# Batch 0's attention placed alone ahead of the products, and the packing of batches 1 to 3 placed inside them

## The chip, the cores and the metric

The kernel runs on one core of one Trainium2 chip. The metric is the device time of one execution in microseconds (us); smaller is better. Engines are named as in the profile: PE (matrix products), DVE (VectorE), ACT (ScalarE), POOL (GpSimd), SP (the queue that issues the DMAs).

## The reference

For 8 batches of 8 heads, 576 positions and 64 channels, an attention in two steps, and behind it two feed-forward layers on the 4608 rows of 512 channels:

```python
def sm_attn(qq, kk, vv):
    s = scale * np.matmul(qq, kk.transpose(0, 1, 3, 2))
    ...
    a = np.exp(s)
    a = a / (np.sum(a, axis=-1, keepdims=True) + 1e-09)
    return np.matmul(a, vv)
p_packed = sm_attn(p, k, v)               # 32 packed positions
out = sm_attn(q, p_packed, p_packed)      # 576 positions out of 32
...
rms = np.sqrt(np.mean(x * x, axis=-1, keepdims=True) + 1e-06)
g = (x / rms * rms_g) @ w_gate
x = (g * sigmoid(g)) * ((x / rms * rms_g) @ w_val) @ w_out
a, b = x @ w1, x @ w2
return (a * b @ w3) @ w_out2
```

(The last lines are put together from two functions; `sigmoid` stands for the expression written out there. The four weights of the second layer and the three of the first arrive as 64-bit floats.)

## The kernel before

**Three stages.** The first runs the attention and the gate and value products of the first layer, batch by batch. The second and third do the products behind them; the change touches nothing there. What moves lies in the first stage, in the first 190 us.

**Pieces of a batch's attention.** `pack(b)` (line 174 on) is the first attention. It is a generator of seven pieces, each ended by `yield`: the scores `k` by `pTs` (L186), maximum (L190) and exponential (L193) of one half of the heads; the same of the other half; the transposes of the exponentials (L202) with the copies into `a1T` (L203 on ACT, L204 on DVE) and the reciprocals of the sums (L205, L206); the product with `v` (L213) and the load of the next `v`; the scaling (L221); a transpose (L225) with the copies into `bdP1T` (L229) and `gP1T` (L231); the small products of `bdP1T` with itself (L239) with four copies into `bdG` (L244). `unpack(b)` is the second attention in eighteen pieces: scores from `q` and `bdP1T` (L267), DVE transposes (L271), maximum, subtraction and exponential (L277 to L280), sums and their reciprocals (L283 to L285), a multiplication on POOL (L286), transposes back into `a2T` (L290), products with `bdG` (L297) and the squares (L300), a sum on POOL (L303), its reduction over partitions by a product with `ones` (L309, read by L311), the reciprocal root `rinv` on POOL (L314, L315), its spread (L320), the scaling of `a2T` (L323) and the split of `a2T` into a rounded part `ah` (L59, ACT) and a remainder `al` (L60, DVE).

**Weights.** `gvw` converts the 24 tiles of the gate and value weights from 64-bit floats, one tile to a step: two operations on ACT (L112, L113), two on DVE (L115 makes `c_t`, L116 writes `wgv`), one on POOL (L118), and a load for the tile three steps ahead (L103). A group g of 256 columns is four tiles; `wb_unit(b, g)` (L342, with its split into `wbh` on ACT and `wbl` on DVE) needs them.

**Products.** `dense_units(b)` is 48 units of six matrix products each (L380) for batch b, with `th` (L386 on ACT, L387 on DVE), `vl` (L391, ACT) and `ht` (L392, POOL) behind them; `wb_unit` for the next group stands behind units 3, 11, 19 and so on. The first unit of batch b needs `ah` and `al` of `unpack(b)` and group 0 of the weights.

**What sets the order.** Each engine works through its own queue in program order, and the program order is written out by hand. In the front, a string names which generator moves on: `p` (pack), `u` (unpack), `c` (a weight tile), `w` (the first `wb_unit`), `l` (loads for later). After it, `planned` runs the 48 units of a batch and moves the other generators on at the unit numbers given in lists: `PACK`, `UNPACK` and one for the weight steps. In the front stand `pack(0)`, `pack(1)`, `unpack(0)` and twelve weight steps; in batch b's products `pack(b + 2)` and `unpack(b + 1)`, in those of batch 0 also the other twelve weight steps, and from batch 1 on five steps a batch of `ow`, the conversion of later weights.

**PSUM.** All pieces of the attention and `wb_unit` share two slots of two banks (`slot("at")`); L380 has four banks of its own (`gv`).

## Time and profile before

| | |
|---|---|
| median of 3 runs | 1374.38 us (1374.08 to 1375.65) |
| the profiled execution | 1373.85 us, its span 1372.1 us |
| mean granted clock of PE | 0.983 |
| PE busy | 1319.5 us, 96% of the span |
| DVE, ACT, POOL busy | 62%, 42%, 44% |

The page is of one execution of the program. Busy time of PE is modelled from pipelined instructions, so a busy PE is not PE at its peak. `x16` behind a row is the number of instructions in it; a product in 32-bit floats counts as two, so L186's 16 products of `pack` are 32 in the trace. An idle time in square brackets stands ahead of the instruction, with what ended it.

### The profile page before, as it was taken

The page shows a single profiled execution, that of the slowest core. Times are in us where ns is not written, and L with a number is a line of the kernel's source. Part 1 is how long each engine was busy: PE and PEld are TensorE (multiplying, and loading weights), DVE is VectorE, ACT ScalarE, POOL GpSimd, SP SyncE. Part 2 cuts the span into 40 slices and gives each one's busy share as a digit, 9 for nine tenths or more (in the row PEclk, how much of TensorE's full clock was granted, in tenths as well). Part 3 has the DMA queues.
Part 4 walks back from the last instruction along what each step waited for, and adds up shares of the span by engine and source line. Part 5 has one row for each costly group of instructions (what it writes and reads, how often), then busy time and mean ns, then how long its engine had stood idle before and what let it go on. Part 6 is the DMA issues. An engine that isn't in the chain of part 4 may idle for free.

```text
span 1372.1 us, 23271 instructions
## 1 busy us (share of the span) xinstructions
PE 1319.5 (96%) x8800; PEld 1118.3 (82%) x8800; DVE 854.9 (62%) x1308; ACT 574.3 (42%) x1093; POOL 608.0 (44%) x524
## 2 busy tenths in 40 slices
PE   4479999999999999999999999999999999999998
PEld 1368888888888888888888888888888888899998
DVE  4787676866867557745376464566467457557444
ACT  2465665655656666534244343015005103304113
POOL 2456556555555653212132113447345544545543
PEclk7699999999999999999999999999999999999999
DMA  9763666564543457743299884756755855787875
GB/s 311 278 242 93 220 208 215 192 193 152 175 146 109 140 178 257 258 144 123 74 334 384 337 303 167 265 207 201 283 194 198 280 209 193 244 311 254 280 269 183
DMA packets 86688, 301.94 MB, mean 220 GB/s; under 512 B 9520, under 2 KB 14640, under 8 KB 72624
## 3 DMA queue, kind: packets, MB, share of 16 engines
q1 hardware_dynamic: 86576, 300.46, 63.3%
q8 instruction: 69, 1.13, 0.3%
q14 instruction: 43, 0.35, 0.1%
HBM read 223.87 MB, written 76.55 MB: 219 GB/s over the span
## 4 chain that ended last, share of the span: by engine, by line
PE 87%; DVE 5%; issue 1%; DMA 1%; POOL 1%; ACT 1%; SPq 0%; ACTq 0%; DVEq 0%; POOLq 0%
PE gv L380 20%; PE gv L878 13%; PE at L878 13%; PE at L567 12%; PE gv L567 7%; PE gv L972 6%; PE at L972 6%; PE gv L668 3%; PE at L342 3%; PE at L297 1%; DVE wgv L116 1%; PE at L213 1%; DMA hr<-hT_d 1%; DVE wbl L60 1%; PE at L309 1%
## 5 line engine op out<-in xcount | busy, mean ns | idle before, releaser
L392 POOL TENSOR_TENSOR ht<-th,vl 128x288 f32<-128x288 f32 x192 | 163.3, 859 | 109.4 <-ACT vl L391 50.0
L380 PE MATMUL gv<-ah,wbh 128*128 128x288 f32 x768 | 175.2, 309 | 2.4 <-ACT vl L391 2.0
L380 PE MATMUL gv<-ah,wbl 128*128 128x288 f32 x768 | 164.7, 296 | 1.8 <-DVE wbl L60 1.8
L380 PE MATMUL gv<-al,wbh 128*128 128x288 f32 x768 | 164.6, 295 | 0.0
L380 PEld LDWEIGHTS gv<-ah,wbh 128*128 128x128 f32 x768 | 121.8, 189 | 50.8 <-issue 24.1
L60 DVE TENSOR_TENSOR hl<-hr,hh 128x512 fp32r<-128x512 f32 x108 | 100.5, 936 | 76.8 <-ACT hh L59 74.7
L904 POOL TENSOR_TENSOR s<-uc 128x512 f32<-128x512 f32 (+1 forms) x40 | 49.0, 1224 | 219.5 <-DVE uc L860 219.5
L118 POOL TENSOR_TENSOR c_o<-c_o,c_y 128x512 int32<-128x512 int32 x52 | 70.8, 1362 | 166.3 <-DVE c_o L116 103.7
L878 PE MATMUL gv<-xh,w 128*128 128x512 f32 (+1 forms) x560 | 137.7, 367 | 0.0
L878 PE MATMUL at<-xh,w 128*128 128x512 f32 (+1 forms) x560 | 137.7, 367 | 0.0
L380 PEld LDWEIGHTS gv<-ah,wbl 128*128 128x128 f32 x768 | 123.3, 188 | 2.9 <-DVE wbl L60 2.9
L380 PEld LDWEIGHTS gv<-al,wbh 128*128 128x128 f32 x768 | 123.6, 189 | 0.0
L387 DVE SCALAR_TENSOR_TENSOR th<-th,gv 128x288 f32<-128x288 f32 x192 | 85.2, 445 | 55.6 <-ACT th L386 51.4
L59 ACT ACTIVATE hh<-hr 128x512 fp32r<-128x512 f32 x108 | 67.7, 629 | 116.3 <-PE at L567 61.0
L878 PEld LDWEIGHTS gv<-xh,w 128*128 128x128 f32 x560 | 102.5, 188 | 13.4
L878 PEld LDWEIGHTS at<-xh,w 128*128 128x128 f32 x560 | 102.5, 188 | 13.3
L567 PE MATMUL at<-hl,wo_h 128*128 128x512 f32 x288 | 112.1, 389 | 0.0
L567 PE MATMUL at<-hh,wo_l 128*128 128x512 f32 x288 | 112.1, 389 | 0.0
L567 PE MATMUL at<-hh,wo_h 128*128 128x512 f32 x288 | 112.0, 389 | 0.0
L391 ACT ACTIVATE vl<-gv 128x288 f32<-128x288 f32 x192 | 79.1, 412 | 75.7 <-PE gv L380 57.0
L386 ACT ACTIVATE th<-gv 128x288 f32<-128x288 f32 x192 | 79.1, 412 | 49.2 <-PE gv L380 47.0
L60 POOL TENSOR_TENSOR xl<-yi,xh 128x1024 fp32r<-128x1024 f32 (+1 forms) x20 | 52.1, 2607 | 74.3 <-ACT xh L59 50.8
(156 smaller groups left out, 2812.7 us busy)
## 6 DMA issues: line engine op xcount, KB each, us to landing
w<-ws_d SPq DMA_DIRECT2D x40, 1024.0 KB, 5.5
w<-w_d SPq DMA_DIRECT2D x35, 1024.0 KB, 4.8
w<-ws_d SPq DMA_DIRECT2D x40, 768.0 KB, 5.9
hT_d<-ht SPq DMA_DIRECT2D x96, 288.0 KB, 3.3
hr<-hT_d SPq DMA_DIRECT2D x108, 256.0 KB, 4.7
w<-in_w_gv_dram SPq DMA_DIRECT2D x24, 512.0 KB, 7.7
w<-in_w_out_dram SPq DMA_DIRECT2D x20, 512.0 KB, 4.7
v<-in_v_dram SPq DMA_DIRECT2D x8, 1152.0 KB, 7.7
```

Of the source, the lines that this page charges most:

```text
L59: nc.scalar.activation(out=hi, in_=src, func=AF.Copy)
L60: eng_lo.tensor_tensor(out=lo, in0=src, in1=hi.bitcast(F32), op=ALU.subtract)
L118: nc.gpsimd.tensor_tensor(out=d, in0=d, in1=shape(y), op=ALU.add)
L380: nc.tensor.matmul(t[:, :HALF], lhsT=w[:, e, 256 * i + 128 * f:256 * i + 128 * f + 128], rhs=x[:, e, HALF * hf:HALF * hf + HALF], start=(n ...
L386: nc.scalar.activation(out=th, in_=t[:, :HALF], func=AF.Tanh, scale=0.5)
L387: nc.vector.scalar_tensor_tensor(out=th, in0=th, scalar=1.0, in1=t[:, :HALF], op0=ALU.add, op1=ALU.mult)
L391: nc.scalar.activation(out=vl, in_=t[:, :HALF], func=AF.Copy, scale=0.5)
L392: nc.gpsimd.tensor_tensor(out=ht[:, hf], in0=th, in1=vl, op=ALU.mult)
L567: nc.tensor.matmul(acc[m], lhsT=w[:, kk, 128 * m:128 * m + 128], rhs=x, start=(kk == 0 and a == 0), stop=(kk == NF - 1 and a == 2))
L878: nc.tensor.matmul(t, lhsT=wi[:, r, pos, a], rhs=x[:, j, r, :w], start=(start and at == 0), stop=(at == 5), skip_group_check=True)
L904: nc.gpsimd.tensor_tensor(out=s2, in0=u2, in1=c22, op=ALU.mult)
L972: nc.tensor.matmul(t, lhsT=wi[:, s, k, 128 * m:128 * m + 128], rhs=x, start=(j in (0, 5, 4, 3) and k == 0 and n == 0), stop=(k == 3 and n ...
```

## The change

Seven things change; what is computed stays the same.

The front's string now moves only `pack(0)`, `unpack(0)`, the first `wb_unit`, the later loads and eight weight steps. `pack(1)` stands in batch 0's products at units 0 to 14, `unpack(1)` behind it at units 13 to 44, and sixteen weight steps at every second unit from 2 to 33. Batch 1's products hold `pack(2)`, `unpack(2)` and `pack(3)` and two steps of `ow`. From batch 2 on, `pack(b + 2)` and `unpack(b + 1)` stand at the same units as before, with six steps of `ow` instead of five.

Copies move: the four into `bdG` from DVE to ACT, and for all batches but 0 the one of `a1T`'s first half too. In `pack`, the reciprocals of the sums stand ahead of the copies. The load of batch 0's `v` is issued ahead of the first three weight tiles. `ones` holds 1/512, so that the mean comes out of L309 and one POOL operation (L314) is gone. An exponential of two elements at the very start brings the load of ACT's table there.

```diff
+    nc.gpsimd.memset(ones, 1.0 / DM)
+    nc.scalar.activation(out=ones[:, 1:], in_=ones[:, :1], func=AF.Exp)
+    nc.gpsimd.memset(ones, 1.0 / DM)
...
-        nc.scalar.activation(out=a1T[:, 1], in_=ts[1][:TP, :R * 128], func=AF.Copy)
-        nc.vector.tensor_copy(a1T[:, 0], ts[0][:TP, :R * 128])
         nc.vector.tensor_scalar(out=rs, in0=rs, scalar1=1e-9, scalar2=None, op0=ALU.add)
         nc.vector.reciprocal(out=rs, in_=rs)
+        if b:
+            nc.scalar.activation(out=a1T[:, 0], in_=ts[0][:TP, :R * 128], func=AF.Copy)
+        else:
+            nc.vector.tensor_copy(a1T[:, 0], ts[0][:TP, :R * 128])
+        nc.scalar.activation(out=a1T[:, 1], in_=ts[1][:TP, :R * 128], func=AF.Copy)
         yield
...
-            nc.vector.tensor_copy(bdG[c0, b % 2, :, c0], t[c0, :, :NP])
+            nc.scalar.activation(out=bdG[c0, b % 2, :, c0], in_=t[c0, :, :NP], func=AF.Copy)
...
-                                scalar1=0.0, scalar2=1.0 / DM, op0=ALU.max, op1=ALU.mult)
-        yield
-        nc.gpsimd.tensor_scalar(out=ssq, in0=ssq, scalar1=1e-6, scalar2=None, op0=ALU.add)
+                                scalar1=0.0, scalar2=1e-6, op0=ALU.max, op1=ALU.add)
+        yield
...
+    load_v(0)
     next(gvw)
-    load_v(0)
     load_q(0)
...
-    front = dict(p=chained(pack(0), pack(1)), u=unpack(0), c=gvw, w=wb_first(), l=later())
-    for x in "pp c c p c pp c pp u c u u p u p u c w u u u c u uu p u c uu l pp c uu c uu pp c l c c":
+    front = dict(p=pack(0), u=unpack(0), c=gvw, w=wb_first(), l=later())
+    for x in "ppp c p c pp u c p uuuu uu u c u c u u w u c u c u l c uuuu":
...
+            others = [([0, 0, 4, 8, 10, 12, 14], pack(1)),
```

**DVE at the start, from batch 0's maxima to the scores of its second attention.** The names: `c_t` and `wgv` are one weight tile's conversion, `p_` the scaled rows, `bdP1T` what the second attention's scores wait for. Before:

```order
L190 TENSOR_REDUCE mx<-at 128x1
L191 TENSOR_SCALAR nb<-mx 128x1
L115 TENSOR_SCALAR c_t<-c_h 128x512
L116 SCALAR_TENSOR_TENSOR wgv<-c_h,c_t 128x2x256
L115 TENSOR_SCALAR c_t<-c_h 128x512
L116 SCALAR_TENSOR_TENSOR wgv<-c_h,c_t 128x2x256
L204 COPY a1T<-at 96x768
...
L221 TENSOR_SCALAR p_248<-at,rs 128x64 x2
L115 TENSOR_SCALAR c_t<-c_h 128x512
L116 SCALAR_TENSOR_TENSOR wgv<-c_h,c_t 128x2x256
L229 COPY bdP1T<-at 64x4x32 x2
```

and now:

```order
L192 TENSOR_REDUCE mx<-at 128x1
L193 TENSOR_SCALAR nb<-mx 128x1
L205 TENSOR_SCALAR rs<-rs 128x2
L206 RECIPROCAL rs<-rs 128x2
L210 COPY a1T<-at 96x768
L115 TENSOR_SCALAR c_t<-c_h 128x512
L116 SCALAR_TENSOR_TENSOR wgv<-c_h,c_t 128x2x256
L115 TENSOR_SCALAR c_t<-c_h 128x512
L116 SCALAR_TENSOR_TENSOR wgv<-c_h,c_t 128x2x256
L226 TENSOR_SCALAR p_240<-at,rs 128x64 x2
L234 COPY bdP1T<-at 64x4x32 x2
```

The copy of `a1T` moved ahead of two conversions, and no conversion stands any more between the scaled rows and `bdP1T`, where the fourth tile stood.

**PE from the scores of batch 0's second attention to the first products of `dense_units(0)`.** Before:

```order
L267 MATMUL at<-q,bdP1T 32x288 x16
L186 MATMUL at<-k,pTs 32x288 x16
L342 MATMUL at<-wgv,gP1T 32x512 x8
L297 MATMUL at<-a2T,bdG 128x288 x4
L202 MATMUL at<-ident,e_319 96x128 x12
L309 MATMUL at<-ones,sq 96x2 x6
L213 MATMUL at<-v,a1T 32x64 x48
L320 MATMUL at<-ident,rinv 128x96 x6
L225 MATMUL at<-ident,p_499 128x128
L239 MATMUL at<-bdP1T 32x32 x8
L380 MATMUL gv<-ah,wbh 128x288 x2
```

and now (line numbers have shifted by up to seven):

```order
L272 MATMUL at<-q,bdP1T 32x288 x16
L244 MATMUL at<-bdP1T 32x32 x8
L302 MATMUL at<-a2T,bdG 128x288 x4
L346 MATMUL at<-wgv,gP1T 32x512 x8
L314 MATMUL at<-ones,sq 96x2 x6
L324 MATMUL at<-ident,rinv 128x96 x6
L384 MATMUL gv<-ah,wbh 128x288 x2
```

Batch 1's five steps (scores, transposes, product with `v`, transpose, small products) left the stretch, and with the last two of them went what stood directly ahead of the first products.

**DVE in the first units of batch 0's products.** Before:

```order
L387 SCALAR_TENSOR_TENSOR th<-th,gv 128x288
L271 STREAM_TRANSPOSE a_600<-at 128x2x288 x2
L277 TENSOR_REDUCE mx_601<-a_600 128x18
L115 TENSOR_SCALAR c_t<-c_h 128x512
L116 SCALAR_TENSOR_TENSOR wgv<-c_h,c_t 128x2x256
L387 SCALAR_TENSOR_TENSOR th<-th,gv 128x288
L279 TENSOR_TENSOR a_600<-a_600,mx_601 128x576
```

and now:

```order
L391 SCALAR_TENSOR_TENSOR th<-th,gv 128x288
L115 TENSOR_SCALAR c_t<-c_h 128x512
L116 SCALAR_TENSOR_TENSOR wgv<-c_h,c_t 128x2x256
L391 SCALAR_TENSOR_TENSOR th<-th,gv 128x288
L226 TENSOR_SCALAR p_683<-at,rs 128x64 x2
L115 TENSOR_SCALAR c_t<-c_h 128x512
L116 SCALAR_TENSOR_TENSOR wgv<-c_h,c_t 128x2x256
```

Here `pack(1)` is at work in the place of `unpack(1)`, and a conversion stands between nearly any two `th`.

## Rows read from the trace of the kernel before

**Rows 1.** The page, 40 slices of the span: busy tenths of PE.

```profile
PE   4479999999999999999999999999999999999998
```

**Rows 2.** Windows: stretch, length, busy PE, PEld, DVE, ACT, POOL; clock, DMA share, GB/s.

```profile
0.00:64.30 64.30, 26.92 (x388) 14.98 (x388) 37.48 (x70) 23.31 (x40) 20.78 (x25) 0.70 0.85 286
64.30:115.10 50.80, 42.04 (x350) 32.25 (x343) 46.38 (x74) 31.30 (x67) 31.66 (x29) 0.94 0.58 211
115.10:133.88 18.78, 18.73 (x261) 16.57 (x261) 12.48 (x26) 9.36 (x20) 11.56 (x14) 1.00 0.44 128
133.88:188.94 55.06, 55.03 (x601) 46.64 (x600) 37.20 (x74) 32.42 (x70) 29.53 (x33) 1.00 0.63 211
```

**Rows 3.** Timeline of the front, batch 0's packing: start, us, engine, line, operation, what it awaited.

```profile
10.42 1.28 ACT L193 ACT_TABLE_LOAD   x1 [10.42 <-DVE nb L191]
...
12.69 2.77 PE L202 MATMUL at<-ident,e 128*96 128x128 f32 x12 [3.36 <-ACT e L193]
...
15.59 1.64 DVE L116 SCALAR_TENSOR_TENSOR wgv<-c_h,c_t 128x512 int32<-128x512 int32 x1
...
17.15 0.94 DVE L204 COPY a1T<-at 96x768 f32<-96x768 f32 x1
...
24.95 0.66 ACT L112 ACTIVATE c_h<-w 128x512 f32<-128x512 f32 x1 [7.53 <-DMA w<-in_w_gv_dram]
...
26.71 0.60 DVE L229 COPY bdP1T<-at 64x128 f32<-64x128 f32 x2
```

**Rows 4.** Timeline of the front, batch 0's second attention up to the first product.

```profile
27.73 2.38 PE L267 MATMUL at<-q,bdP1T 64*32 64x288 f32 x32
...
32.72 1.33 DVE L279 TENSOR_TENSOR a<-a,mx 128x576 f32<-128x576 f32 x1
...
41.12 0.74 DVE L283 TENSOR_REDUCE rs<-a 128x18 f32<-128x576 f32 x1
...
43.85 0.72 DVE L290 STREAM_TRANSPOSE a2T<-a 128x576 f32<-128x576 f32 x1
...
44.72 4.55 PE L297 MATMUL at<-a2T,bdG 128*128 128x288 f32 x8 [7.14 <-DVE a2T L290]
...
50.15 1.40 POOL L303 TENSOR_TENSOR sq<-sq 128x576 f32<-128x576 f32 x1 [2.56 <-DVE sq L300]
...
55.51 1.76 POOL L315 TENSOR_TENSOR rinv<-ssq,mhalf 96x6 f32<-96x6 f32 x1
...
59.37 1.35 ACT L59 ACTIVATE ah<-a2T 128x576 fp32r<-128x576 f32 x2 [3.63 <-DVE a2T L323]
...
60.98 2.49 DVE L60 TENSOR_TENSOR al<-a2T,ah 128x576 fp32r<-128x576 f32 x2
...
63.39 0.60 DVE L229 COPY bdP1T<-at 64x128 f32<-64x128 f32 x2
...
64.30 0.85 PE L380 MATMUL gv<-ah,wbh 128*128 128x288 f32 x2
```

**Rows 5.** Timeline of PE: first products of batch 0's last unit and batch 1's first.

```profile
133.00 0.43 PE L380 MATMUL gv<-ah,wbh 128*128 128x288 f32 x2
...
133.80 0.43 PE L380 MATMUL gv<-ah,wbh 128*128 128x288 f32 x2
```

**Rows 6.** DVE's groups by line, 64.30 to 133.88: count, busy us, mean ns, idle before.

```profile
L116 DVE SCALAR_TENSOR_TENSOR wgv<-c_h,c_t 128x512 int32<-128x512 int32 x14 | 13.9, 995 | 0.5
...
L115 DVE TENSOR_SCALAR c_t<-c_h 128x512 int32<-128x512 int32 x14 | 9.4, 673 | 1.9 <-ACT c_h L112 1.6
```

**Rows 7.** The same view, 133.88 to 409.44, the same operation for later weights.

```profile
L116 DVE SCALAR_TENSOR_TENSOR c_o<-c_h,c_t 128x512 int32<-128x512 int32 x23 | 15.9, 693 | 0.8
```

**Rows 8.** PE's groups by line, 340 to 395, one batch's products: three steps of `pack`.

```profile
L213 PE MATMUL at<-v,a1T 96*32 96x64 f32 x96 | 1.5, 220 | 0.0
L202 PE MATMUL at<-ident,e 128*96 128x128 f32 x12 | 1.5, 273 | 0.0
...
L186 PE MATMUL at<-k,pTs 64*32 64x288 f32 x32 | 1.2, 409 | 0.0
```

More of the change, by code (lines that the diff above doesn't have):

```diff
@@ L164, in packed_attention_swiglu_bilinear @@
     ones = att.tile([128, 2], F32, name="ones")
-    nc.gpsimd.memset(ones, 1.0)
+    nc.gpsimd.memset(ones, 1.0 / DM)
+    nc.scalar.activation(out=ones[:, 1:], in_=ones[:, :1], func=AF.Exp)
+    nc.gpsimd.memset(ones, 1.0 / DM)
     nc.gpsimd.memset(mhalf, -0.5)
@@ L474, in packed_attention_swiglu_bilinear @@
     for b in range(B - 1):
-        others = [(UNPACK, unpack(b + 1))]
-        if b + 2 < B:
-            others.insert(0, (PACK, pack(b + 2)))
         if b == 0:
-            others.append(([1, 3, 5, 9, 12, 14, 18, 20, 22, 26, 28, 30], gvw))
-        else:
-            others.append(([9, 20, 28, 35, 46], some(ow, 5)))
+            others = [([0, 0, 4, 8, 10, 12, 14], pack(1)),
+                      ([13, 17, 18, 19, 20, 23, 24, 26, 27, 30, 31, 32, 34, 36, 40, 40, 43, 44], unpack(1)),
+                      ([2, 5, 7, 9, 11, 13, 15, 17, 19, 21, 23, 25, 27, 29, 31, 33], gvw), ([20], front["l"])]
+        elif b == 1:
+            others = [([0, 0, 5, 10, 12, 14, 16], pack(2)),
+                      ([15, 17, 19, 20, 21, 24, 25, 28, 28, 31, 32, 33, 35, 37, 40, 41, 43, 44], unpack(2)),
+                      ([23, 23, 30, 36, 38, 42, 45], pack(3)), ([27, 46], some(ow, 2))]
+        else:
+            others = [(UNPACK, unpack(b + 1)), ([9, 18, 23, 28, 35, 46], some(ow, 6))]
+            if b + 2 < B:
+                others.insert(0, (PACK, pack(b + 2)))
         planned(dense_units(b), *others)
```

## The prediction

> **What bounds the kernel now.** I read the page's slices first: PE is busy nine tenths or more in all but the first three slices [rows 1]. So behind the first 100 us or so the time is PE's work, and a change there shows only as work that PE has more or less of. The windows cut the start by the program's stages [rows 2]. Up to the first product at 64.30 PE is busy 26.92 of 64.30 us and DVE 37.48: a chain of small steps bounds this stretch, not an engine. In batch 0's products up to the end of its unit 31 (115.10) DVE is busy 46.38 of 50.80 us, 91%, and PE 42.04: here DVE sets the pace. In units 32 to 47 PE is busy 18.73 of 18.78, and in batch 1's products 55.03 of 55.06 us. So three terms decide: how early the first product comes, how long batch 0's products last (before: 64.30 to 133.80 [rows 4, 5], 69.5 us), and what PE has more to do in batch 1 (before: 55.06). All behind it keeps its PE work and moves as one.
>
> **Term 1, the front.** I follow the chain of batch 0 in the new order, with durations of the old one.
>
> To `bdP1T`. ACT's table load, 1.28 us at 10.42 [rows 3], stood ahead of the first exponential; the new two-element exponential has brought it by then. The transposes (L202) can start 1.3 us earlier, at 11.4; they end about 1.3 earlier too, at 14.2 (before 12.69 + 2.77 = 15.5). The DVE copy of `a1T` began only at 17.15, since two conversions stood ahead of it, one of them 1.64 us long [rows 3]; now it follows the transposes of its half and is done when ACT copies the other, until 15.0 (0.8, an estimate from DVE's 0.94). The second half of the product with `v` adds about 0.8, half of L213's 1.5 [rows 8]: 15.8. In DVE's queue two conversions now stand ahead of the scaling. ACT begins them at 15.0; the first two ACT operations take 0.66 each [rows 3], and the two DVE pairs take 1.1 each without a long one and 2.1 with one (L116 at 0.69 [rows 7], or at 1.64 [rows 3], behind 0.43 for L115, an estimate from its mean of 0.67 [rows 6] less what waiting adds). That gives 18.0 to 19.0. Scaling, transpose and copies take about 1.6 more (the copies 0.60 [rows 3], the other two about 0.5 each by the same row): `bdP1T` at 19.6 to 20.6, where before it was done at 27.31. The reason for the old time is the wait of 7.53 us for the fourth weight tile, which landed at 24.95 [rows 3] while its conversion stood ahead of `bdP1T`. That conversion now stands behind batch 0's second exponentials. The load of `v` moves ahead of three tiles on SP, which delays them by one load; they are wanted from 15.0, and I take it that they have landed.
>
> To `rinv`. L267 takes 2.38 [rows 4]: 22.0. Then come DVE's passes, each about 0.73 where nothing disturbs it (0.74 and 0.72 [rows 4]): second transpose, 22.8; one conversion, 1.1; two maxima and two subtractions, of which one may take 1.33 [rows 4], 3.3; the two sums with what belongs to them, 2.7 (41.12 to 43.85 [rows 4]); transpose, conversion, transpose, 2.5: 32.4 without disturbance, 33 with a little. The second half of L297's 4.55 [rows 4], at the low clock of this stretch, is 2.3: 35.5. Square 0.75, POOL's sum 1.40 [rows 4] and the reduction L309, for which I take the 1.2 of L186 [rows 8]: 38.9. Here DVE has `wbl` and the sixth conversion ahead of the small reading, and POOL has the additions of the sixth and seventh tile ahead of `rinv` (1.4 each, taken from the row of its sum); the first can start at 40.5, and I take `rinv` from 43.3 to 45.1 (1.76 [rows 4]); before it began at 55.51. The steps of batch 1 that stood between (its maxima, copies, scores, transposes) are gone, and so is the POOL operation ahead of `rinv`.
>
> To the first product. From the end of `rinv` (57.27) to the end of `ah` (59.37 + 1.35 = 60.72) took 3.45 [rows 4]: 48.5. Before, PE waited 3.6 us longer, since batch 1's `bdP1T` at 63.39 stood behind `al` on DVE, and its small products ahead of L380 on PE. That is gone. **First product at 48.5 instead of 64.30: 15.8 us earlier.** Ends: 45 if no conversion is slowed, 53.5 if each of the eight on the chain takes the long form.
>
> **Term 2, batch 0's products.** `pack(1)` comes into them and `pack(2)` leaves, so PE's work there is the same. DVE's is not. In units 0 to 33 of the new order, against units 0 to 31 of the old: two more conversions (16 instead of 14), at 995 + 673 ns [rows 6] 3.3 us; `al` of batch 0, 2.49 [rows 4], which was done ahead of 64.30 and now starts half a microsecond ahead of the first product, 1.9; scaling, `bdP1T` and `gP1T` of `pack(1)`, 1.4; one `th`, 0.4; less the `a1T` copy, 0.94, and four `bdG` copies, about 0.9, that ACT now does. ACT has room for them: 31.30 of 50.80 us [rows 2]. That makes 46.4 + 5.1 = 51.5 us of DVE, and at the same 91% 56.4 us for units 0 to 33. For units 34 to 47 I take the old 18.78 [rows 2] less two units of 0.80 [rows 5] and less what `pack` had there, L213 1.5 [rows 8] and some 0.6: 15.0. Together 71.4, **1.9 us longer** than 69.5. Ends: 66.5 if DVE never waits; upwards the two rivals below.
>
> **Term 3, batch 1's products.** They hold `pack(2)` too. PE's steps of a pack at full clock are 1.5 + 1.5 + 1.2 [rows 8] and some 0.6 for two small ones: **4.8 us longer**. DVE with 37.20 of 55.06 us [rows 2] has room for the 4 us that `pack` costs it. Should the packed pieces wait for each other, or for a slot of PSUM, PE stops; I allow up to 3.5 us for that. The weight steps moved from batch 1 to the five behind it (one more each, about 1.1 us of DVE) are hidden under PE.
>
> Not on the path: the `memset`s, the constant in `ones`, and L314 of batches 1 to 7, which lie beside PE's work.
>
> **The sum.** -15.8 + 1.9 + 4.8 = -9.1 us. The profiled execution took 1373.85, so 1364.75; the median of the runs is 0.5 above it. I say 1365.0.
>
> **A rule against the change.** L116 took 995 ns on average in batch 0's products and 693 later [rows 6, 7], and 1.64 us in one place of the front [rows 3]: DVE's operation is stretched where POOL is at work beside it. The Trainium skill ("SBUF — State Buffer", Who interferes with whom) has it that a VectorE instruction with two inputs in SBUF and a GpSimd instruction that reads SBUF exclude each other, the later one waiting for the other's whole length. The long form in the rows agrees with it. Batch 0's products now bring 16 conversions at every second unit, each with its POOL addition, beside POOL's `ht`; by that rule they would block each other more often, which is the third rival.
>
> **Rivals.**
> 1. DVE is fed better than before. The weight steps now alternate evenly with the units, and if DVE never waits batch 0's products take 66.5 instead of 71.4; with a front at 46.5, as its lower end allows, the time is 1358. For it: DVE has only small gaps left to lose. Against it: in-order queues.
> 2. The front waits for weights again. One wait like that of 7.53 us [rows 3], on the fourth or a later tile, takes the first product to 56 and the time to 1372.5. For it: the loads were late before. Against it: 286 GB/s on average up to 64.30 [rows 2] bring the 10.6 MB up to the eighth tile (by their shapes five loads of 1.18 MB, `pTs` and eight tiles of 0.52 MB) by about 38, ahead of their use at 41.
> 3. Contention of DVE and POOL. If each of 16 conversions takes the long 1.64 us in place of 0.995, DVE has 10.4 us more, at 91% 11.4: 1376.4, no change by measure.
> 4. Slower: PE waits for weights inside batch 0's products. `wb_unit` behind units 11, 19, 27 and 35 needs tiles whose steps stand only at 9, 17, 25 and 33; before, they were done some ten units ahead. From a step to its tile: 1.3 us on ACT, 1.7 on DVE, 1.4 on POOL, and an operation ahead in each queue, some 6 us, less three units of 0.80: 3.6 us at each of four places, 14.4 in all if DVE has nothing to do meanwhile: 1379. It turns the gain over from 2.3 us at each place. Against it: DVE, the bound there, has other pieces in its queue and works on during the wait, so that most of it is in my 91% already.
>
> **How the numbers follow.** Forecast 0.58, rival 1 0.15, rival 2 0.09, rival 3 0.08, rival 4 0.10. A measurement of this kernel tells about 0.2%, 2.7 us, from no change. Faster by more: nearly all of the forecast, rival 1, a third of rival 2: 0.72. Within: some of the forecast, most of rivals 2 and 3: 0.15. Slower: rival 4 and a part of 3: 0.13. The range of 1357.5 to 1374.5 leaves rival 4 and the worse half of rival 3 out; it holds the forecast with its ends (-19.3 and -3 at best in terms 1 and 2; -10.8 and +3.5 in terms 1 and 3 at worst).
>
> **What would show it.** In the profile of the changed kernel: the first L384 near 48.5 and no wait for a weight's DMA ahead of `bdP1T` (term 1); the first product of batch 1 some 71 us behind it, DVE at nine tenths up to unit 33 (term 2); batch 1's products near 60 us with PE busy throughout (term 3); the same pace from batch 2 on. I am wrong if `rinv` waits for POOL much beyond 43, if PE waits for POOL ahead of L346 for over 2 us at each of the four places, or if L116's mean in batch 0's products goes beyond 1.3 us.

## The result, and the profile after

The kernel after takes 1389.53 us (median; 1388.85 to 1390.29), the kernel before 1374.41 beside it: ratio 1.011, 95% interval 1.0098 to 1.0123. It is **slower by 15 us** where I forecast 9 us faster. The profiled execution spans 1387.1 us.

Line numbers move by four to five: products L384 (before L380), `wb_unit` L346 (L342), `th` L391, `vl` L395, `ht` L396, squares and their sum L302, L305, L308, reduction and root L314, L319, spread L324.

The page's PE slices of after, answering [rows 1]:

```profile
PE   3768999999999999999999999999999999999998
```

Windows of after: stretch, length, busy PE, PEld, DVE, ACT, POOL, then clock, DMA share, GB/s. The first product stands at 49.78, the first of batch 0's unit 34 at 116.30 (the prediction treats units 0 to 33 and 34 to 47 apart), batch 1's first product at 136.22, batch 2's at 202.97.

```profile
0.00:49.78 49.78, 19.34 (x232) 11.28 (x232) 29.98 (x49) 17.38 (x32) 18.09 (x23) 0.72 0.84 292
49.78:116.30 66.52, 52.46 (x466) 37.55 (x467) 49.76 (x78) 37.50 (x79) 34.39 (x32) 0.90 0.61 206
116.30:136.22 19.92, 16.88 (x136) 13.90 (x135) 12.10 (x18) 10.02 (x22) 10.84 (x11) 0.91 0.16 60
136.22:202.97 66.75, 62.64 (x758) 50.90 (x757) 36.45 (x75) 34.36 (x79) 25.46 (x29) 0.97 0.55 170
202.97:258.50 55.53, 55.15 (x600) 46.52 (x599) 39.46 (x74) 36.48 (x81) 32.04 (x35) 1.00 0.65 214
```

The kernel before, over the same units 0 to 33:

```profile
64.30:119.26 54.96, 46.20 (x468) 36.32 (x461) 49.06 (x78) 32.12 (x69) 35.12 (x32) 0.94 0.57 202
```

The front is 14.5 us shorter. Batch 0's products grew from 69.5 to 86.4 us and batch 1's from 55.06 to 66.75; from batch 2 on the pace is the old one. In batch 0's products PE was busy 69.3 us and idle 17.1; before, by [rows 2], 60.8 and 8.8. So of the 16.9 us half is waiting. The other half is PE being busy longer at the same products, and most of it is one line, `wb_unit`'s (after, then before):

```profile
L346 PE MATMUL at<-wgv,gP1T 64*32 64x512 f32 x96 | 13.7, 681 | 9.9 <-POOL wgv L118 9.9
L342 PE MATMUL at<-wgv,gP1T 64*32 64x512 f32 x96 | 6.5, 600 | 3.0 <-DVE a L271 1.9 <-DVE sq L300 1.1
```

Sixteen of its matmuls take 1.09 us when they run together; where a wait splits them, each four alone take 1.05 us or more (rows below). The rest of the 8.6 us, and a part of these 7.2, comes of the clock: means of 0.90 and 0.91 between levels of 1.2 and 2.4 GHz put 17 us of after's stretch at the lower level, against 6 us before, which costs some 5.5 us at most (an estimate from the rows; for a part of that time PE stood still anyway).

PE's waits in batch 0's products of after (total us, times, longest), the first two of the view:

```profile
PE at L346 <- POOL wgv L118: 9.9, 5, 3.0
PE at L314 <- POOL sq L308: 3.0, 1, 3.0
```

The longest of these stops, on the timeline of after (start, us, engine, line, operation; in brackets the idle time before and what ended it):

```profile
98.55 1.06 PE L346 MATMUL at<-wgv,gP1T 64*32 64x512 f32 x8
...
99.04 1.33 POOL L291 TENSOR_TENSOR a<-a,rs 128x576 f32<-128x576 f32 x1
99.40 1.53 DVE L116 SCALAR_TENSOR_TENSOR wgv<-c_h,c_t 128x512 int32<-128x512 int32 x1
...
101.07 1.27 POOL L118 TENSOR_TENSOR wgv<-wgv,c_y 128x512 int32<-128x512 int32 x1 [0.69 <-DVE wgv L116]
...
102.39 1.05 PE L346 MATMUL at<-wgv,gP1T 64*32 64x512 f32 x4 [2.77 <-POOL wgv L118]
...
102.75 1.21 POOL L291 TENSOR_TENSOR a<-a,rs 128x576 f32<-128x576 f32 x1 [0.41 <-DVE rs L290]
102.98 1.52 DVE L116 SCALAR_TENSOR_TENSOR wgv<-c_h,c_t 128x512 int32<-128x512 int32 x1
103.91 1.24 POOL L396 TENSOR_TENSOR ht<-th,vl 128x288 f32<-128x288 f32 x1
...
105.11 1.26 POOL L118 TENSOR_TENSOR wgv<-wgv,c_y 128x512 int32<-128x512 int32 x1
...
106.43 1.92 PE L346 MATMUL at<-wgv,gP1T 64*32 64x512 f32 x4 [3.00 <-POOL wgv L118]
```

Read it from below: PE waits for the last tile's addition; that stands behind `ht`, which is ready earlier, on POOL; the tile's L116 on DVE lasts 1.52 us, where one with POOL idle took 0.69 (after's front, at 16.25); POOL's L291, a piece of the attention, runs beside it. After the wait four matmuls take 1.92 us instead of 1.05, at the lower clock. The trap in these rows: the wait has one name, L118, yet an attention piece, a product's `ht` and the conversion pass through both engines by turns.

### The profile page after: what moved, and what is told of

The parts are those of the page before. It is cut to its first block, busy times and chain, and to the rows that moved or that the text cites. A ratio compares the mean times of both kernels' runs of the same rounds, so it can differ in the third digit from the quotient of the medians.

```text
span 1387.1 us, 23272 instructions
## 1 busy us (share of the span) xinstructions
PE 1328.6 (96%) x8800; PEld 1121.6 (81%) x8800; DVE 845.3 (61%) x1269; ACT 586.8 (42%) x1133; POOL 607.1 (44%) x517
## 4 chain that ended last, share of the span: by engine, by line
PE 87%; DVE 4%; issue 2%; ACT 2%; POOL 1%; DMA 1%; SPq 0%; ACTq 0%; DVEq 0%; POOLq 0%
PE gv L384 20%; PE gv L887 12%; PE at L887 12%; PE at L576 12%; PE gv L576 7%; PE gv L981 6%; PE at L981 6%; PE at L346 3%; PE gv L677 3%; PE at L302 1%; PE at L218 1%; DMA hr<-hT_d 1%; PE at L204 1%; PE at L272 1%; DVE wbl L60 1%
## 5 line engine op out<-in xcount | busy, mean ns | idle before, releaser
L396 POOL TENSOR_TENSOR ht<-th,vl 128x288 f32<-128x288 f32 x192 | 163.3, 856 | 149.4 <-ACT vl L395 97.3
L384 PE MATMUL gv<-ah,wbh 128*128 128x288 f32 x768 | 177.6, 312 | 4.3 <-ACT vl L395 1.8
L384 PEld LDWEIGHTS gv<-ah,wbh 128*128 128x128 f32 x768 | 122.9, 190 | 55.7 <-issue 26.8
L384 PE MATMUL gv<-ah,wbl 128*128 128x288 f32 x768 | 165.4, 297 | 1.8 <-DVE wbl L60 1.8
L384 PE MATMUL gv<-al,wbh 128*128 128x288 f32 x768 | 165.9, 297 | 0.0
L118 POOL TENSOR_TENSOR c_o<-c_o,c_y 128x512 int32<-128x512 int32 x52 | 71.5, 1375 | 155.3 <-DVE c_o L116 105.8
L384 PEld LDWEIGHTS gv<-ah,wbl 128*128 128x128 f32 x768 | 124.2, 190 | 2.8 <-DVE wbl L60 2.8
L384 PEld LDWEIGHTS gv<-al,wbh 128*128 128x128 f32 x768 | 124.8, 190 | 0.3 <-DVE al L60 0.3
L391 DVE SCALAR_TENSOR_TENSOR th<-th,gv 128x288 f32<-128x288 f32 x192 | 85.5, 446 | 62.1 <-ACT th L390 58.0
L395 ACT ACTIVATE vl<-gv 128x288 f32<-128x288 f32 x192 | 78.9, 411 | 77.5 <-PE gv L384 71.2
L60 DVE TENSOR_TENSOR wbl<-at,wbh 128x1024 fp32r<-128x1024 f32 x48 | 58.4, 1218 | 54.6 <-ACT wbh L59 54.6
```

Source lines behind the costliest of these rows:

```text
L60: eng_lo.tensor_tensor(out=lo, in0=src, in1=hi.bitcast(F32), op=ALU.subtract)
L118: nc.gpsimd.tensor_tensor(out=d, in0=d, in1=shape(y), op=ALU.add)
L384: nc.tensor.matmul(t[:, :HALF], lhsT=w[:, e, 256 * i + 128 * f:256 * i + 128 * f + 128], rhs=x[:, e, HALF * hf:HALF * hf + HALF], start=(n ...
L391: nc.vector.scalar_tensor_tensor(out=th, in0=th, scalar=1.0, in1=t[:, :HALF], op0=ALU.add, op1=ALU.mult)
L395: nc.scalar.activation(out=vl, in_=t[:, :HALF], func=AF.Copy, scale=0.5)
L396: nc.gpsimd.tensor_tensor(out=ht[:, hf], in0=th, in1=vl, op=ALU.mult)
```

## The experiments

The first theory was rival 4 of the prediction, weight tiles that come just in time; against it stood the contention of DVE and POOL, then the steps' places, and last a pair of faults of which each is enough.

In the table, beside the times, stand three lengths from each kernel's timeline: the first product; batch 0's products, up to 4.28 us behind the start of batch 1's first `wb_unit` (as it is in after); and batch 1's, from that `wb_unit` to batch 2's. The ratio is against before on the same chip. Each length is that of one profiled execution, and this lies up to 2.3 us from the kernel's median (pool_read's above it, wide's 2.2 below); differences of 2 us between lengths are not resolved.

| kernel | us | ratio, 95% interval | first product | batch 0 | batch 1 |
|---|---|---|---|---|---|
| before | 1374.4 | 1 | 64.3 | 69.5 | 55.1 |
| after | 1389.5 | 1.0110 [1.0098, 1.0123] | 49.8 | 86.4 | 66.3 |
| free_weights | 1389.1 | 1.0112 [1.0097, 1.0127] | 50.0 | 86.8 | 66.2 |
| free_no_add | 1377.4 | 1.0021 [1.0012, 1.0031] | 49.8 | 75.4 | 66.2 |
| pool_write | 1382.4 | 1.0063 [1.0046, 1.0080] | 50.0 | 78.3 | 66.7 |
| pool_read | 1385.4 | 1.0081 [1.0064, 1.0098] | 50.3 | 84.6 | 66.3 |
| pool_wait | 1384.3 | 1.0073 [1.0058, 1.0088] | 50.8 | 80.7 | 66.2 |
| small | 1371.5 | 0.9983 [0.9974, 0.9992] | 61.9 | 69.5 | 55.1 |
| odd_small | 1372.7 | 0.9990 [0.9981, 1.0000] | 62.0 | 70.4 | 55.0 |
| even | 1385.8 | 1.0084 [1.0069, 1.0099] | 50.0 | 85.2 | 66.1 |
| pack2_tail | 1384.3 | 1.0078 [1.0063, 1.0093] | 50.8 | 91.6 | 56.9 |
| even_tail | 1381.2 | 1.0053 [1.0038, 1.0068] | 49.9 | 88.6 | 56.9 |
| roll | 1431.7 | 1.0417 [1.0402, 1.0433] | 49.8 | 86.4 | 60.6 |
| wide | 1386.8 | 1.0095 [1.0078, 1.0112] | 50.1 | 84.1 | 64.7 |
| small16 | 1384.7 | 1.0076 [1.0061, 1.0091] | 60.2 | 83.3 | 55.0 |
| small16_free | 1374.4 | 1.0002 [0.9992, 1.0011] | 59.7 | 73.5 | 55.0 |
| twelve | 1382.4 | 1.0064 [1.0049, 1.0079] | 50.4 | 81.7 | 66.1 |
| best1 | 1425.0 | 1.0370 [1.0355, 1.0386] | 45.0 | 83.9 | 61.5 |
| small2 | 1370.7 | 0.9975 [0.9964, 0.9986] | 57.8 | 71.1 | 55.1 |
| best2 | 1374.7 | 1.0001 [0.9992, 1.0011] | 45.0 | 89.0 | 55.3 |

### Are the weight tiles late, or the additions dear?

**free_weights**: the waiting for tiles taken away, all conversions left.

```diff
+        gs = g if b else 0
-                                 rhs=wgv[..., c, :, 256 * g:256 * g + 256],
+                                 rhs=wgv[..., c, :, 256 * gs:256 * gs + 256],
```

> The changed kernel, but wb_unit of batch 0 reads the tiles of group 0, which are converted long before, for every group (its products with the wrong weights; amount and order of the work are the same, the 16 conversions stay). So PE waits no more for a tile's addition on POOL. Theory A (weights arrive just in time: PE stops ahead of L346, and what feeds DVE and ACT stops with it): batch 0's products fall from 86.4 us to 71 to 76, the time by 10 to 14 us to about 1377. Theory B (DVE is simply overloaded by 16 conversions beside POOL, the waits of PE are a sign of it): batch 0's products stay above 82 us, the time above 1385.

**free_no_add**: the same, and POOL's L118 left out for the sixteen tiles in batch 0's products.

```diff
-        nc.gpsimd.tensor_tensor(out=d, in0=d, in1=shape(y), op=ALU.add)
+        if add:
+            nc.gpsimd.tensor_tensor(out=d, in0=d, in1=shape(y), op=ALU.add)
```

> As free_weights, and POOL's addition (L118) is left out for the 16 tiles converted inside batch 0's products, so that DVE's two operations on a tile meet POOL less often. If contention between DVE and POOL costs time (theory B): L116's mean falls from about 1.04 us to near 0.69, and batch 0's products get shorter than in free_weights by 8 to 10 us. Theory A: DVE has time left once PE no longer waits, and the difference to free_weights is under 3 us.

Without the waits for tiles the length stays (86.8 against 86.4 us). The waiting passes to other names, as the rows of free_weights in 64 to 134 us show (its products are L385):

```profile
PE gv L385 <- DVE th L392: 2.9, 2, 2.6
PE at L272 <- DVE bdP1T L234: 2.7, 1, 2.7
PE at L302 <- DVE a2T L295: 2.5, 1, 2.5
PE at L302 <- DVE wbl L60: 2.2, 1, 2.2
PE at L314 <- POOL sq L308: 2.1, 1, 2.1
```

Taking out the additions, work and not a wait, gives 11.4 us. The windows of batch 0's products (columns as above) and DVE's groups (mean ns) say how much of that is DVE's own time: free_weights, then free_no_add.

```profile
49.99:136.78 86.79, 70.33 (x599) 55.46 (x600) 61.05 (x95) 47.42 (x100) 45.18 (x43) 0.82 0.51 172
...
L116 DVE SCALAR_TENSOR_TENSOR wgv<-c_h,c_t 128x512 int32<-128x512 int32 x16 | 16.7, 1044 | 0.6
...
L115 DVE TENSOR_SCALAR c_t<-c_h 128x512 int32<-128x512 int32 x16 | 10.9, 680 | 8.9 <-ACT c_h L112 8.7
```

```profile
49.77:125.16 75.39, 65.45 (x599) 51.86 (x600) 55.67 (x95) 46.95 (x100) 24.11 (x27) 0.88 0.57 198
...
L116 DVE SCALAR_TENSOR_TENSOR wgv<-c_h,c_t 128x512 int32<-128x512 int32 x16 | 15.3, 956 | 0.5
...
L115 DVE TENSOR_SCALAR c_t<-c_h 128x512 int32<-128x512 int32 x16 | 8.5, 533 | 8.3 <-ACT c_h L112 8.1
```

0.088 + 0.147 us a conversion, 3.8 us for sixteen; all of DVE's work together is 5.4 us shorter. That the other 6 us are queueing is inferred. One rival stands in the first of these rows: free_weights ran at a mean clock of 0.82 here, after at 0.90, so the lower clock might hide a gain. It doesn't: the four executions of free_weights took 1389.1 to 1389.9 us at mean clocks of 0.975 to 0.984 over the whole kernel, and the one with the highest clock, above any of after's, was the longest.

Three kernels put another instruction where the addition stood, each from free_no_add:

```diff
+        else:                                  # pool_write
+            nc.gpsimd.memset(y, 0)
+            nc.gpsimd.memset(y, 0)
+        else:                                  # pool_read
+            nc.gpsimd.tensor_tensor(out=y, in0=y, in1=y, op=ALU.add)
+        else:                                  # pool_wait
+            nc.gpsimd.memset(d, 0)
+            nc.gpsimd.memset(y, 0)
```

> As free_no_add (products of batch 0 read weight group 0 in all groups, GpSimd's addition left out for the 16 conversions inside batch 0; 1377.4), but GpSimd fills the same integer tile twice with zeros (two fills of 128x512) in place of each addition. GpSimd is then occupied about as long as by an addition and holds ScalarE's tile c_y as long, but reads nothing and does not touch the weight tile. Theory B (VectorE's and GpSimd's accesses hinder each other): as free_no_add, 1377 (+-2), or part of the way if writes hinder too. Theory B' (GpSimd's queue: other GpSimd operations and the tile c_y wait while it adds): back to 1386 to 1390.

> As free_no_add, but GpSimd adds the integer tile c_y to itself in place of each of the 16 additions left out: the same kind of instruction on 128x512 elements, reading and writing as much, but it does not wait for VectorE's second conversion operation. Read by the length of batch 0's products (86.4 us in after, 75.2 in free_no_add, 78.3 in pool_write, where GpSimd filled tiles instead). If GpSimd's reading hinders VectorE (theory B): 84 to 87 us. If GpSimd standing still behind VectorE, with everything else in its queue, is what costs (theory B'): 77 to 80.

> As pool_write, but the first of the two fills that replace each addition goes to the weight tile itself, so that it waits for VectorE's second conversion operation as the addition does, and reads nothing (the weights of groups 2 to 5 become zero, so batches 1 to 3 multiply zeros; batch 0 reads group 0 throughout, as in free_no_add, and is the stretch to look at). Theory B' (GpSimd's queue stands still behind VectorE): batch 0's products 83 to 87 us. Theory B (reads): 77 to 80, as pool_write.

Batch 0: no instruction 75.4 us, fills that wait for nothing of DVE 78.3, fills that wait for L116 80.7, an addition that doesn't wait 84.6, the addition that does (free_weights) 86.8. By these lengths POOL's standing still behind DVE costs 2.2 to 2.4 us, additions instead of fills 6.1 to 6.3, being occupied at all 2.9; between the medians of the times it is 1.8 to 3.8, 2.9 to 4.9 and 5.0. So a busy POOL costs time even with fills, and the addition of free_weights costs more than fills in its place (by the intervals both are clear of noise); what standing still costs is not resolved, and neither theory alone has it. A part of the second step is occupancy too, since two fills take 1.07 us and an addition 1.28 to 1.36. L116's mean follows the reading: 956 ns without, 986 and 954 with fills, 1105 with pool_read's additions, though the waiting addition of free_weights shows 1044. The Trainium skill ("SBUF — State Buffer", Who interferes with whom) lets a two-input VectorE instruction collide with a GpSimd instruction that reads and not with one that only writes; these means agree. The rule was in my prediction, as a term of DVE's time. Here DVE's own time was about half of its price.

### Where the steps stand

**small**: before with the small changes of the diff alone, the order untouched.

```diff
+    nc.gpsimd.memset(ones, 1.0 / DM)
+    nc.scalar.activation(out=ones[:, 1:], in_=ones[:, :1], func=AF.Exp)
-            nc.vector.tensor_copy(bdG[c0, b % 2, :, c0], t[c0, :, :NP])
+            nc.scalar.activation(out=bdG[c0, b % 2, :, c0], in_=t[c0, :, :NP], func=AF.Copy)
-        nc.gpsimd.tensor_scalar(out=ssq, in0=ssq, scalar1=1e-6, scalar2=None, op0=ALU.add)
...
```

> The kernel before with the small changes alone (table load at the start, reciprocals ahead of the copies, the bdG copies and a1T's first half on ACT, the constant in ones, v's load ahead of the weights'); the order of pack, unpack and weight steps stays. If the loss lies in the order alone: 1 to 5 us faster than before, 1370 to 1373. If ACT's new copies hurt (a rival for the loss): slower than before.

By the ratio it is 2.3 us faster than before, so the loss is in the order and not in the small changes. **odd_small** and **even** test whether a weight step at an odd unit delays `th`:

```diff
-  ([1, 3, 5, 9, 12, 14, 18, 20, 22, 26, 28, 30], gvw)          # small
+  ([1, 3, 5, 9, 13, 15, 19, 21, 23, 27, 29, 31], gvw)          # odd_small
-  ([2, 5, 7, 9, 11, ..., 31, 33], gvw)                         # after
+  ([2, 4, 6, 8, 10, ..., 30, 32], gvw)                         # even
```

> The kernel small (the kernel before with the small changes alone, 1371.5) with its twelve weight steps of batch 0's products all at odd units (1, 3, 5, 9, 13, 15, 19, 21, 23, 27, 29, 31 instead of 1, 3, 5, 9, 12, 14, 18, 20, 22, 26, 28, 30). Theory D: each of the seven that change places delays TensorE by 0.6 to 1 us, so 1375 to 1379. Theory B: the same as small, 1371.5 +- 2.

> The kernel after, with the weight steps of batch 0's products at units 2, 4, 6, ..., 32 instead of 2, 5, 7, ..., 33: the same 16 conversions, one unit earlier nearly throughout. Theory D (place in the order): at an odd unit the first ScalarE copy of a conversion stands behind the copy vl of that unit's sums, which waits for TensorE, and VectorE does the conversion's two operations before it can do the next unit's th; at an even unit they stand behind th, whose bank has already been freed, and a unit without a VectorE operation of its own comes next. By D batch 0's products fall from 86 us by 8 to 12, the kernel to 1378 to 1381. Theory B (VectorE and GpSimd hinder each other while both work on a conversion, wherever it stands): batch 0's products within 3 us of 86, the kernel 1387 to 1390.

D forecast 3.5 to 7.5 us in small's order and 8.5 to 11.5 in after's. There were 1.2, which the intervals don't resolve, and 3.7, which they barely do; the length of batch 0 shows 1.2 of these, in an execution that was even's second longest. Theory D fell as the main cause.

### Batch 1

**pack2_tail** gives batch 2's packing to the end of batch 0's products, and before's lists to batch 1; **even_tail** does both that and even.

```diff
+                      ([34, 35, 38, 40, 42, 45, 46], pack(2))]
         elif b == 1:
-            others = [([0, 0, 5, ..., 16], pack(2)), ([15, 17, ..., 44], unpack(2)),
-                      ([23, 23, 30, 36, 38, 42, 45], pack(3)), ([27, 46], some(ow, 2))]
+            others = [(PACK, pack(3)), (UNPACK, unpack(2)), ([27, 46], some(ow, 2))]
```

> The changed kernel, with pack(2) at the end of batch 0's products (units 34 to 46) instead of in batch 1's, whose lists are those of the kernel before. If batch 1's loss of some 7 us beyond a pack's 4.8 us comes from two packs and an unpack crowded into one batch: batch 1's products take 55 to 56 us, batch 0's 86.4 + 5 to 8, the time falls by 3 to 7 us to 1383 to 1387. If not: the time stays within 2 us of 1389.5.

> The kernel even, with batch 2's packing in the last 14 units of batch 0's products and, in batch 1, the lists of places that the kernel before has (batch 3's packing and batch 2's unpacking). Moving that packing out of batch 1 gave 5.3 us in the kernel after (batch 1's products 56.9 us, batch 0's some 5 more). If theory D and the crowding of batch 1 are two separate losses, both gains add up: 1372 to 1376. If they are one loss (work that is pushed out of one stretch waits in the next), 1383 to 1386.

Batch 1 returns to 56.9 us, batch 0 pays 5.2 of it. even_tail lies between its two forecasts: its gain of 8.3 us is nearly the 3.7 and 5.3 of its two parts. **roll** gives every batch from 1 on its own pack and unpack, at after's units for batch 1:

```diff
+            others = [([0, 0, 5, 10, 12, 14, 16], pack(b + 1)),
+                      ([15, 17, 19, 20, 21, 24, 25, ..., 44], unpack(b + 1)), ...]
```

> The kernel after with one packing and one unpacking in each of batches 0, 1 and 2 (batch b holds pack(b+1) and unpack(b+1)) instead of two packings in batch 1 and none in batch 2. If batch 1's excess of 11.7 us over before is the second packing's 4.8 us of TensorE work plus waits that come of the crowding, batch 1 falls to 56 to 60 us and batch 2 (55.5 us, TensorE busy for all of it) grows by the packing's 4.8 us at most: 1381 to 1385. If a packing together with its own unpacking in one batch already costs the waits, without a second packing: 1387 to 1391.

Far off, and the expectation itself was wrong: batches 2 to 5 of after do hold a packing, `pack(b + 2)`, so roll changed the spacing in five batches, 2 to 6. That made it the clearest run. Batch 1 with one packing fewer is 5.7 us shorter, and still 5.6 longer than before's, which has the same pieces. In batches 2 to 5 the pieces are as many as in after, only closer, and the second attention follows its own packing within the batch: 64.4 to 65.1 us instead of 55.6 to 56.1. PE's waits in roll's batch 2, some two thirds of the difference (PE is also busy longer there, at a clock of 0.97); the first three of the view, then the rows that lead to the longest:

```profile
PE gv L384 <- ACT vl L395: 2.3, 1, 2.3
PE at L314 <- POOL sq L308: 1.4, 1, 1.4
PE at L302 <- DVE a2T L295: 1.2, 1, 1.2
```

```profile
228.68 1.39 DVE L284 TENSOR_TENSOR a<-a,mx 128x576 f32<-128x576 f32 x1
...
230.11 0.68 ACT L285 ACTIVATE a<-a 128x576 f32<-128x576 f32 x1 [3.14 <-DVE a L284]
...
231.44 0.53 PE L384 MATMUL gv<-ah,wbh 128*128 128x288 f32 x2 [2.35 <-ACT vl L395]
```

In before, six to eight units lie between the transposes of `a2T` and the squares' matmuls, the sum and its reduction, `rinv` and its spread; in roll two to three. PE works in program order, gets there first and stops: the second and third of the waits. The longest comes through ACT, which works in order too: ACT stood idle 3.14 us ahead of the exponential L285, for DVE's subtraction, and behind it in ACT's queue stood `th` and the `vl` that frees the bank of a later product. So batch 1's 11.3 us in after are 5.7 for the second packing and 5.6 for the close spacing.

### Number, lead or spacing of the steps in batch 0

**wide** spreads batch 1's attention in after and changes nothing else; **twelve** moves five weight steps into after's front and leaves eleven in batch 0, at before's units, which changes number and lead together; **small16** does the reverse to small; **small16_free** is small16 with the edit of free_weights, so that no product waits for a late tile. (The kernel before has thirteen weight steps in the front and eleven in batch 0's products, not twelve and twelve; the last of the twelve places there finds no tile left.)

```diff
-  [0, 0, 4, 8, 10, 12, 14], pack(1)                            # after
+  [0, 0, 3, 5, 6, 8, 10], pack(1)                              # wide
-  [13, 17, 18, 19, 20, 23, 24, 26, 27, 30, 31, 32, 34, 36, 40, 40, 43, 44], unpack(1)
+  [11, 12, 13, 14, 15, 17, 18, 19, 20, 25, 25, 26, 31, 32, 40, 41, 42, 44], unpack(1)
-  "... w u c u c u l c uuuu"                                   # after
+  "... w u c u c u c l c uu c uu c c c"                        # twelve
-  "... p u c uu l pp c uu c uu pp c l c c"                     # small
+  "... p u c uu l pp uu uu pp l"                               # small16
```

> The kernel after with other unit numbers for batch 1's attention inside batch 0's products, nothing else: pack(1) at 0, 0, 3, 5, 6, 8, 10 and unpack(1) at 11 to 44 with the late gaps of the kernel before (squares at 25 behind the transposes at 19 and 20, the reduction over partitions at 31 behind the sum at 26, the spread of rinv at 40 behind rinv at 32; in after these gaps are 3, 2 and 4 units). Theory W (TensorE, which works in program order, reaches each step of the attention before VectorE and GpSimd have its input): batch 0's products fall from 86.4 us by 6 to 12, the kernel to 1378 to 1384. Theory C (the number of conversions and additions in the stretch decides): within 3 us of 86.4, the kernel 1387 to 1391.

> The kernel small (the kernel before with the small changes; order of before, thirteen weight steps in the front) with only eight weight steps in the front and sixteen in batch 0's products, at the units of after. Theory C: batch 0's products grow from small's 69.5 us to 80 or more, as in after, though the attention steps stand as in before; the kernel 1378 to 1385. Theory W: batch 0's products 70 to 75 us, the front no longer, the kernel 1370 to 1375.

> The kernel after with thirteen weight steps in the front, the last three behind the split as in before, and the other eleven in batch 0's products at the units of before; pack(1) and unpack(1) stay at the units of after. Theory C: batch 0's products fall from 86.4 us to 70 to 75. Theory W: they stay at 80 or more. The front grows by either theory, by the additions that stand ahead of its late steps: first product at 51 to 55 us instead of 49.8. Kernel by C 1377 to 1383, by W 1386 to 1392.

> small16 (order of before, sixteen weight steps in batch 0's products), but batch 0's products read weight group 0 in all groups, as free_weights does in after's order; the conversions all stand and run as in small16. In small16 each group's last tile was due two units behind its step, in before four to ten, and TensorE waited 12.3 us for GpSimd's additions in batch 0's products (83.3 us). Theory J (two faults, each of which alone is enough: tiles due two units behind their step, and attention steps spaced too narrowly): here only the second could act and is absent, so batch 0's products fall to 69 to 74 us, the kernel to 1370 to 1376. Theory C (the number of weight steps in the stretch, whatever they are waited for): 81 to 84 us, the kernel 1382 to 1386, as free_weights left after unchanged.

Neither W nor C holds: wide gives back 2.3 us (not resolved: its interval overlaps after's), twelve 4.7, and small16 loses 13.8 with spacing untouched. It isn't the amount of work either. small2 (below) does as much in a stretch 12 us shorter; windows of small16 and of small2 over batch 0's products, columns as above:

```profile
60.15:143.47 83.32, 69.14 (x605) 51.79 (x600) 62.44 (x93) 47.50 (x103) 45.30 (x43) 0.91 0.54 174
```

```profile
57.83:128.89 71.06, 63.07 (x599) 49.99 (x600) 61.62 (x95) 47.20 (x100) 45.01 (x43) 0.91 0.63 214
```

DVE is busy 62.4 and 61.6 us, POOL 45.3 and 45.0. What differs is the lead: in small16, as in after, a group's last tile is converted two units before `wb_unit` wants it, in small2 five to ten units. small16's first wait says so, and with that wait gone (small16_free) batch 0 falls to 73.5 us:

```profile
PE at L346 <- POOL wgv L118: 12.3, 6, 3.2
```

So with the order of before, a lead of two units costs 9.8 us. With the order of after the same edit gave nothing.

### Three versions

**best1** is roll (whose loss was not known when it was planned) with even's places and, in the front, the conversions ahead of `rinv` put behind it; **small2** makes that move in small; **best2** is after with best1's front, wide's spacing, a lead of seven to ten units, and batch 2's packing spread in batch 0 (22 to 43).

```diff
-  "ppp c p c pp u c p uuuu uu u c u c u u w u c u c u l c uuuu"    # after
+  "ppp c p c pp u c p uuuu uu u c u c u u w u u u l c u u c u u c" # best1, best2
-  "... u uu p u c uu l pp c uu c uu pp c l c c"                    # small
+  "... u uu p u uu l pp c uu pp uu c c l"                          # small2
-  [2, 5, 7, 9, ..., 33], gvw                                       # after
+  [0, 1, 2, 3, 4, 5, 7, 9, 12, 14, 16, 18, 20, 22, 26, 28], gvw    # best2
```

> roll, with even's places for batch 0's weight steps, and in the front the three conversions that stand ahead of rinv (GpSimd's power of batch 0's row sums) put behind it and behind the steps after it. In after, rinv started 3.8 us after its sums, behind two additions; taking these away should bring the first product from 49.8 to 45 to 47 us. Gains by themselves: even 3.7 (measured), roll 4.5 to 8.5 (expected), front 3 to 4.7. If they add: 1372 to 1378. If batch 0 is bounded by VectorE and GpSimd together, so that the earlier start is waited away: 1376 to 1381.

> The kernel small with the end of its front in another order: the conversions that stand between the sum of squares and rinv, and between the scaling of a2T and its split, go behind these; pack(1)'s last two steps go ahead of the split; three conversions go into batch 0's first units. In best1 the same move brought the first product from 49.8 to 45.0 us. Here: first product 57 to 59 us instead of 61.9; batch 0's products 69.5 to 72 with the three conversions more. If the earlier start holds: 1367 to 1370. If batch 0 takes it back: 1371 to 1373.

> The kernel after with both faults of theory J mended in batch 0 and the two losses beside it: batch 1's attention at the wide spacing of wide; sixteen weight steps at 0, 1, 2, 3, 4, 5, 7, 9, 12, 14, 16, 18, 20, 22, 26, 28, so that each group's last tile has seven to ten units; batch 2's packing at 22 to 43 of batch 0's products and before's lists in batch 1; the front of best1 (first product at 45.0 us). Theory J: batch 0's products 72 to 78 us in spite of the packing more in them, batch 1's 55 to 58, the kernel 1359 to 1367. Theory C: batch 0's products 84 to 90 us, the kernel 1372 to 1378.

The front's move is real: best1's `rinv` starts at once behind its sums, and the first product comes 4.8 us earlier than in after.

```profile
40.48 0.16 DVE L316 TENSOR_SCALAR ssq<-at 96x6 f32<-96x6 f32 x1 [0.20 <-PE at L314]
...
40.78 1.40 POOL L319 TENSOR_TENSOR rinv<-ssq,mhalf 96x6 f32<-96x6 f32 x1 [1.98 <-DVE ssq L316]
...
45.02 1.27 PE L384 MATMUL gv<-ah,wbh 128*128 128x288 f32 x2 [1.56 <-ACT ah L59]
```

small2 is the fastest version, 3.4 us ahead of before; its first product is 4.1 us earlier than small's, and batch 0 takes 1.5 of that back. Its lead over small itself is not resolved, since the intervals overlap. best2 met the numbers of theory C, not J: batch 1 is at 55.3 us, but batch 0 takes 89.0. Its windows, the first 43 us, the worst piece, and the end:

```profile
44.99:87.75 42.76, 31.95 (x342) 23.97 (x342) 34.47 (x53) 25.09 (x52) 21.55 (x19) 0.81 0.67 226
87.75:110.97 23.22, 15.27 (x118) 11.06 (x117) 19.74 (x33) 13.63 (x30) 15.30 (x14) 0.85 0.63 217
110.97:133.99 23.02, 23.02 (x299) 19.84 (x300) 12.32 (x27) 13.59 (x31) 11.25 (x13) 1.00 0.36 106
```

Up to 110.97 DVE is busy 82% and PE 72%; then PE works without a gap. Batch 0's products end at 134.0 us, as they do in before (133.8), though they start 19 us sooner. In the other versions too an earlier start doesn't show in the end: with a first product at 45 to 51 us the ends of batch 0's products lie at 128.9 to 142.4 in the kernels that compute everything, and small2, which starts at 57.8, ends at 128.9.

Of best2's 19 us of waiting, no tile of the weights has a part. Three rows of PE's waits there point elsewhere:

```profile
PE at L188 <- DVE wbl L60: 4.4, 1, 4.4
PE at L346 <- ACT a1T L208: 3.2, 2, 2.6
PE at L302 <- ACT e L195: 1.3, 1, 1.3
```

None of these matmuls reads what it waits for. `wbl`, `a1T` and `e` are each made from a PSUM tile of `slot("at")`, and the next matmul of the attention or of `wb_unit` needs one of its two slots. twelve has 7.9 us of such waits, before itself 6.5 of its 8.8. No run changes the number of slots, so this rival of lead and spacing stands untested.

## Why the prediction was wrong

**Term 1 was right.** First product at 49.78, forecast 48.5; `bdP1T` was done at 20.85 (forecast 19.6 to 20.6) and `rinv` began at 45.16 (43.3), behind two additions as foreseen. From its end to the first product it took 2.8 us in place of 3.45, which hides 0.6 us of that delay:

```profile
20.24 0.61 DVE L234 COPY bdP1T<-at 64x128 f32<-64x128 f32 x2 [0.70 <-PE at L230]
...
45.16 1.79 POOL L319 TENSOR_TENSOR rinv<-ssq,mhalf 96x6 f32<-96x6 f32 x1
...
49.78 1.27 PE L384 MATMUL gv<-ah,wbh 128*128 128x288 f32 x2 [1.56 <-ACT ah L59]
```

Rival 2 didn't come; ACT waited once for a tile's load, 3.25 us until 33.54, well behind `bdP1T`.

**Term 2 failed, by 15.0 us, at the words "at the same 91%".** In units 0 to 33 the work was sized well: DVE was busy 49.76 us, where I had 51.5 (before, over the same units, 49.06). The rate was not: these units took 66.52 us instead of 56.4, so DVE was busy 75% of them. That is 10.1 of the 15.0 us. The other 4.9 lie in units 34 to 47, 19.9 us instead of 15.0, where I had PE working without a stop at the full clock: PE stood 3.0 us ahead of L314 for POOL's sum, which is placed two units before it, and the mean clock was 0.91.

I had taken a share that an old, loosely spaced order reaches [rows 2] for a property of the engine. Two things can let it down, and the runs show each in another order: tiles due two units after their step (small16 less small16_free, 9.8 us) and attention pieces too close for engines that work in program order (roll, 8 to 9 us a batch). In after both are there, together with the additions of POOL, and mending one leaves the others: no weights to wait for, 0; even places, 1.2 us of batch 0, and spacing, 2.3, both near the noise; fewer and earlier weight steps, 4.7. How the 15 us divide among them is not settled, and the cause in after's order stays open. best2, with lead and spacing mended at once, should have settled it and did not: it carries another packing, starts 5 us sooner, and waits for the two PSUM slots. The ends of batch 0's products might suggest that DVE's and POOL's work up to that point sets them. Against it stand small16 and small16_free, with 62.4 and 63.2 us of DVE and 45.3 and 45.6 of POOL in batch 0's products, which end 10 us apart.

**Rival 4 has the right number by the wrong mechanism.** 71.4 + 14.4 = 85.8 us against 86.4, and PE did wait 9.9 us for POOL ahead of L346, near the sign that I had named (over 2 us at each of four places; it was 1.8, 2.3, 5.8 and nothing). Taking the waiting away left the time as it was. By free_weights' waits, what was wrong is not that "DVE works on during the wait": the pieces that it works on are ones for which PE then stops further down. A matching figure isn't a cause.

**Rival 3 was half right.** L116's mean was 1.043 us, far from 1.64, and the additions lengthen DVE's own work by 5.4 us. They cost 11.4.

**Term 3 was short by 6.5 us.** The packing's price was right: in before, a batch with one takes 55.6 us or a little more, the one without 50.7, so 4.9 us against my 4.8. I allowed up to 3.5 us for pieces waiting for each other and put none of it into the sum; it was 5.6, and the second packing cost 5.7 in place of 4.8.

The three errors, 1.3 + 15.0 + 6.5, make 22.8 of the 24.5 us by which I missed. 0.6 more lies in batches 2 to 6 and about 1 us I did not trace.

## What to carry to other kernels

When work moves in a hand-written order, don't carry the busy share along with it: count for each piece how many steps lie between its producer and the in-order engine that reads it, before and after, and price every distance that shrinks. To learn whether a wait is the cause, take it away and look at the total; if the total stays, the names in the list of waits are only who came last, and taking out work tells more. An earlier start is worth only what the stretch behind it doesn't take back: of small2's 4.1 us, 1.5 were lost again.
